# Experts in descending order of their token counts, with falling widths, and one addition on GpSimd instead of VectorE

## The chip, the cores and the metric

The kernel runs on one core of a Trainium2 chip. The metric is the device time of one execution in microseconds; where several executions were timed, their median. A profiled execution also gives a trace: its span runs from the first to the last instruction, and its own time is a little longer than the span.

In this text PE is TensorE, DVE is VectorE, ACT is ScalarE, POOL is GpSimd, and SP is the engine whose queue issues most of the DMAs.

## What is computed

The reference has three stages. A linear attention over 4 sequences of 768 tokens gives 3072 rows of 384 numbers. A mixture of eight experts follows: each token goes to the one expert with the largest gate value. A gated feed-forward layer over all tokens ends it.

```python
def _moe_ref(x, w_gate, w_output_gate, w1, w2):
    e_idx = np.argmax(x @ w_gate, axis=1)
    ...
    for e in range(E):                      # E = 8
        mask = e_idx == e
        h = np.maximum(x[mask] @ w1[e], 0.0)    # 384 -> 1024
        ye = h @ w2[e]                          # 1024 -> 384
        out[mask] = gate_w[mask, None] * eom[mask, e, None] * ye

def _moe2_ref(x, w_gate, w_val, w_out):     # 384 -> 1536 -> 384
    g = x @ w_gate
    silu = g * (1.0 / (1.0 + np.exp(-g)))
    return (silu * (x @ w_val) @ w_out).astype(np.float32)
```

How many tokens an expert gets depends on the data. With the inputs of the reference the counts of experts 0 to 7 are 380, 348, 359, 410, 409, 389, 374 and 403.

## The kernel before

Every float32 product is made of three products of a high and a low part (type fp32r): a low by a high, a high by a low, a high by a high. So each weight and each activation is split: ACT casts the high part, DVE subtracts it from the value and has the low part.

**Attention and routing** (0 to about 131 us). The tokens pass in 24 tiles of 128. `route` finds each token's expert and its place in that expert's list, in groups of six tiles; the last group (18 to 23) is routed when the attention is over. Its result is `rows`, 8 x 4 columns of token numbers, four columns of 128 places for each expert.

**The head** (`MoE.head`, about 130 to 150 us). Expert 0's first 256 tokens come from the first 18 tiles, so its work on them starts while the last group is still routed. It runs in eight steps `f`, one for each 128 of the 1024 hidden units: nine matmuls into `pha`, ACT and DVE make `h` (high and low) of it, and two steps later nine matmuls take `h` into `pya`. `pha` has two PSUM buffers. The small DVE work of the routing stands in the same DVE queue.

**The experts** (`MoE.run`, about 150 to 372 us). Expert 0's other 160 columns come first, then experts 1 to 7 in the order of their numbers, each over `CAP` = 416 columns whatever its count: eight steps of nine matmuls into `ph` and nine into `py`, 144 in all. Beside them each expert needs its weights loaded by SP and split (`load` and `prefetch`, three groups ahead), and its tokens gathered by POOL and transposed on PE (`gather`, `transposed`: four tiles of up to 128 tokens, three transposes each). The last layer's weights arrive as 64-bit floats; `widen` turns 36 chunks of them into float32 in three stages, six chunks during each of experts 1 to 6. In a chunk, line 973 clamps, line 975 makes an exponent, line 978 shifts, line 979 (POOL) multiplies, line 981 (DVE) adds, and line 982 puts the sign in. `sorted_positions` works out where each expert's list starts (`off_f`, `offs`) and the order of the tokens for the output.

**The feed-forward layer** (`FFN`, 372 us to the end) runs over seven blocks of sorted tokens and scatters each finished tile to its tokens by an indirect DMA.

**What sets the order.** In the attention and the head PE, DVE, ACT and POOL follow the order that is written in the code, though a scheduler may put work of the later part between. From `MoE.run` on a scheduler places the instructions. Each engine and the SP queue then works in the order of its own queue. If an expert has more tokens than its columns, `rest` computes them after the end, which these counts don't ask for.

Of the kernel before, what the change touches and what calls it, by code (L numbers as in the profile page):

```python
# [27 lines left out]

HEAD = 256
# [7 lines left out]
def moe_kernel(ctx, tc, cst, small, tok, tr, u, w1, w2, m_gate, m_val, m_out, out):  # L37
# [14 lines left out]
    assert CAP < NJ * P  # L52
# [11 lines left out]
    ident, mask, iota_p, niota, rev8, slot, tokid, tile_i, part_i, ltm = (  # L64
        cs[:, at[n]] for n in ("ident", "mask", "iota", "niota", "rev", "slot", "tokid", "tile", "part", "ltm")
    )
    ltm = ltm.rearrange("p (a b) -> p a b", a=E)
# [11 lines left out]
    rows_h = const.tile([P, 2], I32, name="rows_h")  # L79
    offs = const.tile([P, E], I32, name="offs")  # L80
# [46 lines left out]
    def route(sl, lg, mx, pool, ps, sm):  # L127
# [84 lines left out]
        nc.vector.tensor_tensor(out=rows if sl.stop == NTILE else rows_f, in0=rows_f, in1=psw[:, 1, :], op=ALU.add)  # L212

    def gate(sl, lg, mx, pool, sm):
# [43 lines left out]
        nc.vector.tensor_tensor(out=scale3[:, 2, sl], in0=s1, in1=scale3[:, 1, sl], op=ALU.subtract)  # L258

# [4 lines left out]
    with ExitStack() as actx:  # L264
# [305 lines left out]
        with tc.manual_schedule(engines=set(engines)):  # L570
# [62 lines left out]
            moe.gather(0, more, rows[:, HEAD // P : NJ], NT)  # L633
# [8 lines left out]
    def sorted_positions(pool, pool_ps):  # L642

        psn = pool_ps.tile([P, 2, E], F32, name="psn", tag="pd")
        nc.tensor.matmul(psn[:, 0, :], lhsT=ones_b, rhs=cum[:, NTILE, :], start=True, stop=True)
        nc.tensor.matmul(psn[:, 1, :], lhsT=ones_b, rhs=cum[:, NTILE - NCH, :], start=True, stop=True)
        nc.vector.tensor_copy(cnt_f, psn[:, 0, :])
        nc.vector.scalar_tensor_tensor(
            out=again, in0=psn[:, 1, 0:1], scalar=float(HEAD), in1=wide, op0=ALU.is_lt, op1=ALU.max
        )  # L650

        def ins(t, n, at):
            if at == 1:
                return t.rearrange("p (o e) -> p o e", o=1).to_broadcast([P, n, t.shape[1]])
            return t.rearrange("p (e o) -> p e o", o=1).to_broadcast([P, t.shape[1], n])

        pre = pool.tile([P, E, E], F32, name="pre")
        nc.vector.tensor_tensor(out=pre, in0=ltm, in1=ins(cnt_f, E, 1), op=ALU.mult)
        nc.vector.reduce_sum(off_f, pre, axis=AX.X)

        nc.vector.tensor_copy(offs, off_f)
        nc.vector.tensor_scalar(out=offs[:, E - 1 :], in0=off_f[:, E - 1 :], scalar1=float(FFN.NB), scalar2=None, op0=ALU.max)
        nc.vector.scalar_tensor_tensor(
            out=again, in0=off_f[:, E - 1 :], scalar=float(FFN.NB), in1=again, op0=ALU.is_lt, op1=ALU.max
        )
        yield
        most = pool.tile([P, 1], F32, name="most")
        nc.vector.reduce_max(most, cnt_f, axis=AX.X)
        nc.vector.scalar_tensor_tensor(out=rest_i, in0=most, scalar=float(CAP), in1=again, op0=ALU.is_gt, op1=ALU.max)
# [14 lines left out]
        nc.vector.tensor_copy(dlof, dlo)  # L684
# [14 lines left out]
        for i in range(NTILE):  # L699
            doh = pool.tile([P, P], BF16, name="doh", bufs=4)  # L700
            nc.vector.tensor_scalar(out=doh, in0=iota_p, scalar1=dlof[:, i : i + 1], scalar2=None, op0=ALU.is_equal)
# [25 lines left out]
    def sequential(c):  # L727
# [55 lines left out]
        for _ in gate(slice(0, NTILE), lg, mx, sq, scratch(sq)):  # L783
            pass
        for _ in sorted_positions(sq, ps_m):
            pass

    def rest(c):
# [130 lines left out]
class MoE:  # L919
    def __init__(self, tc, c, env):  # L920
# [9 lines left out]
        self.raws, self.xs = {}, {}  # L930
# [9 lines left out]
    def widen(self):  # L940
# [19 lines left out]
        for i in range(n):  # L960
# [20 lines left out]
            nc.vector.tensor_tensor(out=low, in0=ab, in1=low, op=ALU.add)  # L981
# [8 lines left out]
    def load(self, e, g):  # L990
        nc, env, GF = self.nc, self.env, 2
        r1 = self.raw.tile([P, env["KD"], GF * P], F32, name="r1")
        nc.sync.dma_start(out=r1, in_=self.w1v[e, :, :, g * GF * P : (g + 1) * GF * P])
        r2 = self.raw.tile([P, GF, env["DM"]], F32, name="r2")
        nc.sync.dma_start(out=r2, in_=self.w2v[e, :, g * GF : (g + 1) * GF, :])
        self.raws[e, g] = r1, r2
# [11 lines left out]
    def run(self, sorted_positions, gates, ffn):  # L1008
# [26 lines left out]
        for e in range(E):  # L1035
            x, _ = self.xs.pop(e)
            sl = slice(0 if e else HEAD, CAP)
            py = [p_y.tile([P, CAP], F32, name=f"py{d}") for d in range(KD)]
            for f in range(KF):
# [27 lines left out]
                if f == 3 and e + 1 < E:  # L1067
                    load_x(e + 1, range(NJ))
# [3 lines left out]
    def gather(self, e, tiles, rows, last):  # L1072
# [8 lines left out]
        for i, j in enumerate(tiles):  # L1081
            n = min(P, CAP - j * P)
# [5 lines left out]
    def transposed(self, e, tiles, p_t, tag=None):  # L1088
# [4 lines left out]
        for j in tiles:  # L1093
            n = min(P, CAP - j * P)
# [64 lines left out]
    def second(self, after=None):  # L1159
# [7 lines left out]
        if f == KF - 1:  # L1167
            to = sl
            if e:
# [3 lines left out]
                yd, to = yd[:, :, least:], bass.ds(off - least, env["CAP"])  # L1173
# [158 lines left out]
PREFETCH = (7, 10, 13, 16, 19)  # L1332
# [20 lines left out]
def _const_slices():  # L1353
    at = 0
    for name, width in (("ident", P), ("mask", P), ("iota", P), ("niota", P), ("rev", 8), ("slot", 32), ("tokid", 24), ("tile", 24), ("part", 1), ("ltm", 64)):
        yield name, slice(at, at + width)
        at += width
# [5 lines left out]
def _constants():  # L1363
# [6 lines left out]
    c[:, at["iota"]] = np.arange(P)  # L1370
# [3 lines left out]
    c[:, at["tokid"]] = P * np.arange(24) + np.arange(P)[:, None]  # L1374
    c[:, at["tile"]] = np.arange(24)
    c[:, at["part"]] = np.arange(P)[:, None]
    c[:, at["ltm"]] = np.tril(np.ones((8, 8)), -1).reshape(-1)
# [67 lines left out]
```

## Time and profile before

| | us |
|---|---|
| median of 3 runs | 830.68 |
| lowest and highest | 829.99 and 833.25 |
| profiled execution, its own time | 830.09 |
| profiled execution, its span | 828.2 |
| PE busy in the span | 800.0 |
| DVE busy | 516.8 |
| ACT busy | 350.1 |
| POOL busy | 213.8 |

The mean granted clock of PE was 0.992 of full speed. A busy time is the time covered by instructions of an engine; matmuls overlap each other, and the record of one is longer than its distance from the next. The shares of busy time are averages over stages with different limits, so a table by stage (busy times between given moments) stands behind them. The 1.9 us between span and own time are taken as unchanged.

### The profile page before, as it was taken

How to read it: one execution, taken by the hardware profiler on the slowest of the kernel's cores; microseconds unless marked ns; L12 is line 12 of the kernel's file. 1: busy time of each engine (PE TensorE's matmuls, PEld its weight loads, DVE VectorE, ACT ScalarE, POOL GpSimd, SP SyncE). 2: the span in 40 equal slices, each digit the busy share in tenths (PEclk: the TensorE clock that was granted, in tenths of full speed). 3: DMA queues.
4: the chain of work that ended last, by engine and by line, in shares of the span. 5: the costliest groups of instructions: out<-in, count | busy, mean ns of one | idle time of the engine just before them, and what ended most of it. 6: DMA issues, size and time to landing. Idle time of an engine off the chain costs nothing.

```text
span 828.2 us, 15486 instructions
## 1 busy us (share of the span) xinstructions
PE 800.0 (97%) x5991; PEld 728.2 (88%) x5992; DVE 516.8 (62%) x1096; ACT 350.1 (42%) x794; POOL 213.8 (26%) x210
## 2 busy tenths in 40 slices
PE   7989789998999999999999999999999999999997
PEld 4878678997999999998888888888888888889997
DVE  7789996699999999855554335433533533344443
ACT  5878764565556567543432212212322222222321
POOL 6999952546333422200001000200010020001000
PEclk9999999999999999999999999999999999999999
DMA  8999974576778886332210000100010010001000
GB/s 326 305 366 327 333 239 148 157 224 186 242 237 263 253 233 216 107 120 86 86 58 33 19 1 13 39 1 0 13 39 1 1 44 1 1 8 39 1 20 24
DMA packets 61843, 99.63 MB, mean 120 GB/s; under 512 B 5364, under 2 KB 47872, under 8 KB 61760
## 3 DMA queue, kind: packets, MB, share of 16 engines
q1 hardware_dynamic: 58320, 88.44, 32.8%
q0 software_dynamic: 3440, 10.11, 3.7%
q8 instruction: 49, 0.80, 0.4%
q14 instruction: 34, 0.28, 0.1%
HBM read 82.00 MB, written 16.53 MB: 119 GB/s over the span
## 4 chain that ended last, share of the span: by engine, by line
issue 58%; DVE 12%; PE 8%; DMA 3%; POOL 3%; ACT 0%; POOLq 0%; SPq 0%; DVEq 0%; ACTq 0%
PE ph L1131 3%; PE py L1131 3%; POOL out_dram L1275 2%; DVE w1l L1006 2%; DVE h L1151 1%; DVE ab L978 1%; DMA m<-ab 1%; DVE ab L982 1%; DVE ab L973 1%; DMA r<-in_w_dram 1%; DVE low L981 1%; DVE w2l L1006 1%; PE pya L1131 1%; DVE exw L975 1%; PE pha L1131 1%
## 5 line engine op out<-in xcount | busy, mean ns | idle before, releaser
L1304 DVE TENSOR_TENSOR hv<-pg,hv 128x512 f32<-128x512 f32 (+1 forms) x84 | 51.7, 615 | 155.0 <-ACT hv L1303 154.9
L1275 POOL DMA_INDIRECT out_dram<-ot,tokd x24 | 24.9, 1035 | 450.5 <-DVE ot L1274 446.9
L1303 ACT ACTIVATE hv<-pg 128x512 f32<-128x512 f32 (+1 forms) x84 | 45.1, 537 | 167.8 <-PE pg L1299 167.6
L914 ACT CAST hh<-hv 128x512 fp32r<-128x512 f32 (+1 forms) x84 | 47.0, 559 | 141.8 <-DVE hv L1305 141.8
L1266 PE MATMUL po<-wh,hh 128*128 128x384 f32 x288 | 97.1, 337 | 0.0
L1266 PE MATMUL po<-wh,hl 128*128 128x384 f32 x288 | 97.0, 337 | 0.0
L1266 PE MATMUL po<-wl,hh 128*128 128x384 f32 x288 | 96.8, 336 | 0.0
L1131 PE MATMUL ph<-x,w1h 128*128 128x416 f32 x336 | 91.4, 353 | 0.0
L1299 PE MATMUL pg<-xh,wh 128*128 128x512 f32 (+1 forms) x252 | 91.1, 362 | 0.0
L1299 PE MATMUL pg<-xh,wl 128*128 128x512 f32 (+1 forms) x252 | 90.9, 361 | 0.0
L1299 PE MATMUL pv<-xh,wh 128*128 128x512 f32 (+1 forms) x252 | 90.8, 360 | 0.0
L1299 PE MATMUL pv<-xh,wl 128*128 128x512 f32 (+1 forms) x252 | 90.7, 360 | 0.0
L1299 PE MATMUL pv<-xl,wh 128*128 128x512 f32 (+1 forms) x252 | 90.6, 360 | 0.0
L1299 PE MATMUL pg<-xl,wh 128*128 128x512 f32 (+1 forms) x252 | 90.5, 359 | 0.0
L1131 PE MATMUL py<-h,w2h 128*128 128x416 f32 x336 | 88.1, 352 | 0.0
L915 DVE TENSOR_TENSOR hl<-hv,hh 128x512 fp32r<-128x512 f32 (+1 forms) x84 | 51.7, 616 | 45.4 <-ACT hh L914 45.1
L1305 DVE TENSOR_TENSOR hv<-pv,hv 128x512 f32<-128x512 f32 (+1 forms) x84 | 51.7, 615 | 44.1 <-PE pv L1299 43.7
L979 POOL TENSOR_TENSOR low<-low,exw 128x384 f32<-128x384 f32 x36 | 43.5, 1208 | 103.1 <-DVE exw L975 90.9
L440 ACT ACTIVATE dsb<-cs,cb 128x128 f32<-128x128 f32 x192 | 58.8, 388 | 24.7 <-DVE cb L436 24.7
L1131 PEld LDWEIGHTS ph<-x,w1h 128*128 128x128 f32 x336 | 63.5, 190 | 0.7
L1131 PEld LDWEIGHTS py<-h,w2h 128*128 128x128 f32 x336 | 62.9, 188 | 0.9
L1131 PE MATMUL ph<-x,w1l 128*128 128x416 f32 x168 | 61.0, 363 | 0.6 <-DVE h L1151 0.6
(230 smaller groups left out, 1709.5 us busy)
## 6 DMA issues: line engine op xcount, KB each, us to landing
r<-in_w_dram SPq DMA_DIRECT2D x64, 384.0 KB, 4.5
yd_all<-in_tr_dram SPq DMA_DIRECT2D x24, 512.0 KB, 4.8
yd_all<-in_tok_dram SPq DMA_DIRECT2D x24, 384.0 KB, 6.6
m<-ab SPq DMA_DIRECT2D x36, 192.0 KB, 4.1
rw<-m SPq DMA_DIRECT2D x36, 192.0 KB, 2.5
yd_all<-in_tok_dram SPq DMA_DIRECT2D x24, 256.0 KB, 7.4
x_d<-xt SPq DMA_DIRECT2D x24, 192.0 KB, 2.4
cva<-in_w_gate_dram SPq DMA_DIRECT2D x12, 384.0 KB, 3.5
```

Source lines behind the costliest of these rows:

```text
L440: nc.scalar.mul(dsb[:, h, :], ident, cb[:, h : h + 1])
L914: first = nc.scalar.copy(hi, src)
L915: second = nc.vector.tensor_tensor(out=lo, in0=src, in1=hi.bitcast(F32), op=ALU.subtract)
L979: nc.gpsimd.tensor_tensor(out=low, in0=low, in1=ex.bitcast(F32), op=ALU.mult)
L1006: nc.vector.tensor_tensor(out=lo, in0=r, in1=hi.bitcast(F32), op=ALU.subtract)
L1131: nc.tensor.matmul(dst[:, 0:n], lhsT=a, rhs=b, start=start and t == 0, stop=stop and t == 2)
L1266: mm = nc.tensor.matmul(po[t], lhsT=a[:, t * P : (t + 1) * P], rhs=bb, start=(f == 0 and j == 0), stop=(f == KF2 - 1 and j == 2))
L1275: st = nc.gpsimd.indirect_dma_start(out=out[:, :], out_offset=bass.IndirectOffsetOnAxis(ap=tokd[:, i : i + 1].bitcast(U32), axis=0), in_=o ...
L1299: nc.tensor.matmul(dst, lhsT=a[:, fs], rhs=bb[:, q, :], start=(q == 0 and j == 0), stop=(q == KD - 1 and j == 2))
L1303: nc.scalar.activation(hv, pg, AF.Sigmoid)
L1304: nc.vector.tensor_tensor(out=hv, in0=pg, in1=hv, op=ALU.mult)
L1305: nc.vector.tensor_tensor(out=hv, in0=pv, in1=hv, op=ALU.mult)
```

## The change

Each of experts 1 to 7 gets its turn by its count: the largest first. Expert 0 stays first. The turns have the fixed widths `CAPS` = 416, 416, 412, 404, 392, 384, 372, 360 (the first is expert 0's), so the turn is known when the program is built and the expert in it only when it runs. A turn of 384 columns or fewer has three tiles of tokens instead of four.

`in_order`, new, runs after the last group's routing: it ranks the counts and makes `ids` (which expert has which turn), and a selection matrix `pm`. `sorted_positions` uses `pm` to put `rows` and `offs` in the order of the turns and to check the counts against the widths. `load` reads `ids` into a register of SP and addresses the weights by it; the prefetch of the first group of expert 1 in the attention is dropped (`PREFETCH` has four entries instead of five). The constants lose 200 columns. In `widen` the addition (line 981 before) is issued on GpSimd.

```diff
+CAPS = (416, 416, 412, 404, 392, 384, 372, 360)
...
-        nc.vector.tensor_tensor(out=rows if sl.stop == NTILE else rows_f, in0=rows_f, in1=psw[:, 1, :], op=ALU.add)
+        if sl.stop == NTILE:
+            sl0 = slice(HEAD // P, NJ)
+            nc.vector.tensor_tensor(out=rows_m, in0=rows_f[:, sl0], in1=psw[:, 1, sl0], op=ALU.add)
+        nc.vector.tensor_tensor(out=rows_f, in0=rows_f, in1=psw[:, 1, :], op=ALU.add)
...
+    def in_order(pool, psn):
+        nc.tensor.matmul(psn[:, 0, :], lhsT=ones_b, rhs=cum[:, NTILE, :], start=True, stop=True)
...
+        nc.vector.tensor_tensor(out=ahead, in0=ins(rank8, E, 1), in1=ins(rank8, E, 2), op=ALU.is_gt)
+        at_k = pool.tile([P, E], F32, name="at_k")
+        nc.vector.reduce_sum(at_k, ahead, axis=AX.X)
+        nc.vector.tensor_tensor(out=pm, in0=ins(tile_i[:, 0:E], E, 2), in1=ins(at_k, E, 1), op=ALU.is_equal)
...
+        nc.vector.tensor_copy(ids, ids_f)
...
-            moe.gather(0, more, rows[:, HEAD // P : NJ], NT)
+            moe.gather(0, more, rows_m, NT)
+            in_order(acst, in_bank("psn", 2, E))
...
+        each = pool.tile([P, E, NJ, E], F32, name="each")
...
+        nc.vector.reduce_sum(rows_k.rearrange("p (k j) -> p k j", j=NJ), each, axis=AX.X)
+        nc.vector.tensor_copy(rows, rows_k)
...
-            nc.vector.tensor_tensor(out=low, in0=ab, in1=low, op=ALU.add)
+            nc.gpsimd.tensor_tensor(out=low, in0=ab, in1=low, op=ALU.add)
...
+        if e and g == 0:
+            self.ids[e] = bass.ds(nc.sync.value_load(env["ids"][0:1, e : e + 1], min_val=0, max_val=env["E"] - 1), 1)
+        pe = self.ids[e]
         r1 = self.raw.tile([P, env["KD"], GF * P], F32, name="r1")
-        nc.sync.dma_start(out=r1, in_=self.w1v[e, :, :, g * GF * P : (g + 1) * GF * P])
+        nc.sync.dma_start(
+            out=r1, in_=self.w1v[pe, :, :, g * GF * P : (g + 1) * GF * P].rearrange("o p k f -> (o p) k f")
+        )
...
-            sl = slice(0 if e else HEAD, CAP)
+            sl = slice(0 if e else HEAD, CAPS[e])
...
-                    load_x(e + 1, range(NJ))
+                    load_x(e + 1, range(-(-CAPS[e + 1] // P)))
...
-                yd, to = yd[:, :, least:], bass.ds(off - least, env["CAP"])
+                yd, to = yd[:, :, least:], bass.ds(off - least, n)
...
-PREFETCH = (7, 10, 13, 16, 19)
+PREFETCH = (7, 10, 13, 16)
```

Three places show how the queues change. The first is DVE's queue in the head, behind the last group's routing. `h<-pha` is the low part of a step's `h`; `w2l` and `w1l` are low parts of weights; `den`, `key`, `exo`, `gs`, `sc`, `scale` belong to the gate. Before:

```order
L232 RECIPROCAL reo<-key 128x48
L1151 SCALAR_TENSOR_TENSOR h<-pha,h 128x256
L1006 TENSOR_TENSOR w2l<-r_1726,w2h 128x768
L229 TENSOR_REDUCE den<-ex 128x6
L237 TENSOR_TENSOR key<-ex,reo 128x48
L234 TENSOR_SCALAR den_2780<-den 128x6
L1151 SCALAR_TENSOR_TENSOR h<-pha,h 128x256
L242 TENSOR_TENSOR exo<-key,oh_all 128x48
```

Now, the end of the stretch between the same reciprocal and the same `h`:

```order
L285 TENSOR_TENSOR pick<-pm,cs 128x64
L684 TENSOR_TENSOR each<-pm,rows_f 128x256
L263 TENSOR_TENSOR s_2811<-sc,scale_66 128x6
L287 TENSOR_REDUCE ids_f<-pick 128x8
L691 TENSOR_REDUCE rows_k<-each 128x32
L265 CAST scale_66<-s_2811 128x6
L288 CAST ids<-ids_f 128x8
L289 COPY cnt_f<-bank 128x8
L290 SCALAR_TENSOR_TENSOR again<-bank,wide 128x1
L1201 SCALAR_TENSOR_TENSOR h<-pha,h 128x256
L692 CAST rows<-rows_k 128x32
```

Twenty-two instructions stand between the reciprocal and `h` now and none stood there before; ten more stand between that `h` and the next, among them the split `w2l`.

The second place is DVE's queue while expert 4 is computed; `ab<-ab` are lines 973 and 978, `exw` is line 975, `low<-ab,low` the addition, `ab<-cva,low` line 982, and `doh` belongs to the order of the tokens. Before:

```order
L1151 SCALAR_TENSOR_TENSOR h<-ph,h 128x416
L978 TENSOR_SCALAR ab<-ab 128x384
L1006 TENSOR_TENSOR w2l<-r_3716,w2h 128x768
L981 TENSOR_TENSOR low<-ab,low 128x384
L973 TENSOR_SCALAR ab<-ab 128x384
L982 SCALAR_TENSOR_TENSOR ab<-cva,low 128x384
L975 TENSOR_SCALAR exw<-ab 128x384
L978 TENSOR_SCALAR ab<-ab 128x384
```

Now (lines 973, 975, 978 and 982 have become 1018, 1020, 1023 and 1027):

```order
L1201 SCALAR_TENSOR_TENSOR h<-ph,h 128x392
L1018 TENSOR_SCALAR ab<-ab 128x384
L1020 TENSOR_SCALAR exw<-ab 128x384
L1023 TENSOR_SCALAR ab<-ab 128x384
L1006 TENSOR_TENSOR w2l<-r_3879,w2h 128x768
L1201 SCALAR_TENSOR_TENSOR h<-ph,h 128x392
L745 TENSOR_SCALAR doh<-cs,dlof 128x128
L1027 SCALAR_TENSOR_TENSOR ab<-cva,low 128x384
```

The addition is gone from the queue (it stands in POOL's, behind the multiplication of the same chunk), and three other instructions stand here between the shift and line 1027, which waits for it.

The third place is SP's queue at the end of the attention; `yd_all<-in_tok_dram` loads a tile of the attention, `r` are an expert's weights, `cva` the 64-bit weights. Before:

```order
L993 DMA r_2007<-in_w_dram 128x3x256
L995 DMA r_2009<-in_w_dram 128x2x384
L993 DMA r_2753<-in_w_dram 128x3x256
L995 DMA r_2755<-in_w_dram 128x2x384
L993 DMA r_2757<-in_w_dram 128x3x256
L995 DMA r_2759<-in_w_dram 128x2x384
L304 DMA yd_all<-in_tok_dram 128x512
```

Now:

```order
L998 DMA cva<-in_w_out_dram 128x768
L1038 TENSOR_LOAD ids
L1038 ISA x2
L1041 ISA
L1041 DMA r_2771<-in_w_dram 128x3x256
L1045 ISA
L1045 DMA r_2773<-in_w_dram 128x2x384
```

Six loads of expert 1 that stood ahead of the last attention load stand behind the read of `ids` now, which comes after the whole attention, with two more behind them.

## Rows read from the trace of the kernel before

**Rows 1.** The page: span, and busy time by engine
```profile
span 828.2 us, 15486 instructions
PE 800.0 (97%) x5991; PEld 728.2 (88%) x5992; DVE 516.8 (62%) x1096; ACT 350.1 (42%) x794; POOL 213.8 (26%) x210
```

**Rows 2.** Busy time of each engine in the turns of experts 1 to 7
```profile
core 0: us, PE busy (x) PEld busy (x) DVE busy (x) ACT busy (x) POOL busy (x), PEclk, DMA share, GB/s
166.40:199.00 32.60, 32.49 (x181) 30.92 (x179) 32.24 (x61) 18.44 (x38) 15.95 (x13) 1.00 0.64 196
199.00:229.50 30.50, 27.82 (x141) 26.71 (x140) 26.75 (x54) 17.52 (x34) 12.14 (x10) 0.94 0.78 247
229.50:259.40 29.90, 29.90 (x167) 28.50 (x167) 28.44 (x59) 18.40 (x37) 11.69 (x11) 1.00 0.79 253
259.40:288.70 29.30, 29.30 (x166) 28.01 (x165) 29.02 (x60) 16.92 (x34) 11.59 (x11) 1.00 0.82 246
288.70:317.50 28.80, 28.80 (x162) 27.44 (x161) 27.58 (x61) 19.10 (x37) 7.14 (x7) 1.00 0.79 238
317.50:345.60 28.10, 28.10 (x155) 27.50 (x154) 26.78 (x53) 17.34 (x34) 7.63 (x8) 1.00 0.50 149
345.60:371.60 26.00, 26.00 (x140) 25.78 (x139) 15.92 (x29) 13.31 (x27) 1.59 (x2) 1.00 0.42 128
```

**Rows 3.** Timeline of PE (start, us, instruction): nine of 416, nine of 256, six transposes
```profile
361.77 0.35 PE L1131 MATMUL ph<-x,w1l 128*128 128x416 f32 x1
...
363.46 0.92 PE L1131 MATMUL py<-h,w2h 128*128 128x416 f32 x4
...
142.16 0.28 PE L1131 MATMUL pha<-x,w1l 128*128 128x256 f32 x1
...
143.22 0.28 PE L1131 MATMUL pya<-h,w2l 128*128 128x256 f32 x1
...
152.13 0.82 PE L1097 MATMUL pt<-cs,xg 128*128 128x128 f32 x6
152.71 0.40 PE L1127 MATMUL ph<-x,w1h 128*128 128x320 f32 x1
```

**Rows 4.** DVE by line, 259.4 to 288.7 us: busy us, mean ns, idle before
```profile
L1151 DVE SCALAR_TENSOR_TENSOR h<-ph,h 128x416 fp32r<-128x416 f32 x9 | 5.2, 581 | 0.0
L978 DVE TENSOR_SCALAR ab<-ab 128x384 int32<-128x384 int32 x7 | 4.7, 675 | 0.1
...
L981 DVE TENSOR_TENSOR low<-ab,low 128x384 f32<-128x384 f32 x6 | 3.3, 548 | 0.1
...
L975 DVE TENSOR_SCALAR exw<-ab 128x384 int32<-128x384 int32 x6 | 2.1, 351 | 0.0
```

**Rows 5.** Timeline of POOL and DVE around one multiplication
```profile
341.87 1.12 POOL L979 TENSOR_TENSOR low<-low,exw 128x384 f32<-128x384 f32 x1 [3.11 <-DVE exw L975]
342.04 0.58 DVE L1151 SCALAR_TENSOR_TENSOR h<-ph,h 128x416 fp32r<-128x416 f32 x1
342.54 1.27 DVE L1006 TENSOR_TENSOR w2l<-r,w2h 128x768 fp32r<-128x768 f32 x1
```

**Rows 6.** Timeline of DVE: an `h` of the head, two small dependent steps
```profile
139.60 0.41 DVE L1151 SCALAR_TENSOR_TENSOR h<-pha,h 128x256 fp32r<-128x256 f32 x1
...
150.64 0.22 DVE L658 TENSOR_TENSOR pre<-cs,cnt_f 128x64 f32<-128x64 f32 x1
150.90 0.22 DVE L659 TENSOR_REDUCE off_f<-pre 128x8 f32<-128x64 f32 x1
```

**Rows 7.** A wait of PE after expert 1, and the microsecond behind it
```profile
203.73 0.54 PE L1131 MATMUL py<-h,w2l 128*128 128x416 f32 x1 [2.10 <-ACT yd_all L1175]
...
204.00:205.00 1.00, 1.00 (x4) 0.94 (x4) 1.00 (x4) 1.00 (x3) 1.00 (x1) 0.50 0.93 320
```

**Rows 8.** The page's row of the weight loads; a register load on SP
```profile
r<-in_w_dram SPq DMA_DIRECT2D x64, 384.0 KB, 4.5
...
L906 SPq TENSOR_LOAD <-rest_i x1: 472/472/472, 176.2 to 176.2; - x1
```

More of the change, by code (lines that the diff above doesn't have):

```diff
@@ L51, in moe_kernel @@
     NJ = -(-CAP // P)
-    assert CAP < NJ * P
+    assert CAP < NJ * P and CAP == max(CAPS) and len(CAPS) == E
     G = 2 * E
@@ L63, in moe_kernel @@
     at = dict(_const_slices())
[L64 to L65 removed]
+    ident, mask, niota, rev8, slot, tile_i, part_i, lead, caps = (
+        cs[:, at[n]] for n in ("ident", "mask", "niota", "rev", "slot", "tile", "part", "lead", "caps")
     )
[L67 removed]
     mask_b = const.tile([P, P], BF16, name="mask_b")
@@ L79, in moe_kernel @@
     rows_h = const.tile([P, 2], I32, name="rows_h")
+    rows_m = const.tile([P, NJ - HEAD // P], I32, name="rows_m")
+    ids = const.tile([P, E], I32, name="ids")
+    ahead = const.tile([P, E, E], F32, name="ahead")
+    pm = const.tile([P, E, E], F32, name="pm")
+    cap_f = const.tile([P, E], F32, name="cap_f")
     offs = const.tile([P, E], I32, name="offs")
@@ L652, in ins @@
[L652 to L662, printed above, removed]
@@ L663, in sorted_positions @@
-        nc.vector.scalar_tensor_tensor(
-            out=again, in0=off_f[:, E - 1 :], scalar=float(FFN.NB), in1=again, op0=ALU.is_lt, op1=ALU.max
+        pre = pool.tile([P, E, E], F32, name="pre")
+        nc.vector.tensor_tensor(out=pre, in0=ahead, in1=ins(cnt_f, E, 1), op=ALU.mult)
+        nc.vector.reduce_sum(off_f, pre, axis=AX.X)
+        each = pool.tile([P, E, NJ, E], F32, name="each")
+        nc.vector.tensor_tensor(
+            out=each,
+            in0=pm.rearrange("p k (o e) -> p k o e", o=1).to_broadcast([P, E, NJ, E]),
+            in1=rows_f.rearrange("p (o e j) -> p o j e", o=1, j=NJ).to_broadcast([P, E, NJ, E]),
+            op=ALU.mult,
+        )
@@ L667, in sorted_positions @@
+        nc.vector.reduce_sum(cap_f, caps_e, axis=AX.X)
+        over = pool.tile([P, E], F32, name="over")
+        nc.vector.tensor_tensor(out=over, in0=cnt_f, in1=cap_f, op=ALU.subtract)
         most = pool.tile([P, 1], F32, name="most")
-        nc.vector.reduce_max(most, cnt_f, axis=AX.X)
-        nc.vector.scalar_tensor_tensor(out=rest_i, in0=most, scalar=float(CAP), in1=again, op0=ALU.is_gt, op1=ALU.max)
+        nc.vector.reduce_max(most, over, axis=AX.X)
+        nc.vector.scalar_tensor_tensor(out=rest_i, in0=most, scalar=0.0, in1=again, op0=ALU.is_gt, op1=ALU.max)
@@ L784, in sequential @@
             pass
+        in_order(sq, ps_m.tile([P, 2, E], F32, name="psn", tag="m"))
         for _ in sorted_positions(sq, ps_m):
@@ L929, in __init__ @@
         self.pend = []
-        self.raws, self.xs = {}, {}
+        self.raws, self.xs, self.ids = {}, {}, {0: slice(0, 1)}
         self.first = ExitStack()
@@ L1354, in _const_slices @@
     at = 0
-    for name, width in (("ident", P), ("mask", P), ("iota", P), ("niota", P), ("rev", 8), ("slot", 32), ("tokid", 24), ("tile", 24), ("part", 1), ("ltm", 64)):
+    for name, width in (("ident", P), ("mask", P), ("niota", P), ("rev", 8), ("slot", 32), ("tile", 24), ("part", 1), ("lead", 8), ("caps", 8)):
         yield name, slice(at, at + width)
@@ L1373, in _constants @@
     c[:, at["slot"]] = P * np.arange(32)
-    c[:, at["tokid"]] = P * np.arange(24) + np.arange(P)[:, None]
     c[:, at["tile"]] = np.arange(24)
     c[:, at["part"]] = np.arange(P)[:, None]
-    c[:, at["ltm"]] = np.tril(np.ones((8, 8)), -1).reshape(-1)
+    c[:, at["lead"]] = [2**16, *range(-1, -8, -1)]
+    c[:, at["caps"]] = CAPS
     return c
```

48 lines of the change are left out of this document (34 added, 14 removed).

## The prediction, on record before the result

> **What bounds the kernel now.** I read the page first: PE is busy for 800.0 of 828.2 us, DVE for 516.8 [rows 1]. That says PE, but the shares hide where DVE is full, so I read the busy times by turn next. While experts 2 to 6 are computed DVE is busy for 26.75 to 29.02 us of turns of 28.1 to 30.5 [rows 2]: in expert 4's turn it is idle for 0.28 us, in 3's for 1.46, in 5's for 1.22, in 6's for 1.32. PE is covered all the time in 3 to 7. So both engines bound this stretch, and a saving on one of them alone comes only as far as the other has room. Expert 7's turn is different: DVE is busy there for 15.92 of 26.0 us. Behind it the feed-forward layer isn't touched by the change.
>
> What a turn costs PE is read from its timeline [rows 3]. Nine matmuls of 416 columns take from 361.77 to 363.46, 0.1878 us each; nine of 256 columns take 1.06 us, 0.1178 each. The difference, 0.0700 us over 160 columns, is 0.4375 ns a column. Six transposes take 0.58 us, 0.097 each.
>
> **The narrower turns.** A turn has 144 matmuls, so a column less saves 144 x 0.4375 ns = 0.063 us. Turns 2 to 7 lose 4, 12, 24, 32, 44 and 56 columns: 0.25, 0.76, 1.51, 2.02, 2.77 and 3.53 us, 10.84 in all. Turns 5, 6 and 7 have one tile less, three transposes each, done one turn earlier: 0.29 us in each of turns 4, 5 and 6, 0.87 in all. PE has 11.71 us less to do. Turn 1 keeps its 416 columns.
>
> **The addition on GpSimd.** DVE loses an instruction of 0.548 us six times in a turn [rows 4]. That isn't clear profit. The shift of line 978 runs beside POOL's multiplication and takes 0.675 us on the mean, where line 975, of the same kind and size, takes 0.351 [rows 4]: POOL's work delays DVE. One multiplication shows which instructions it delays [rows 5]. POOL runs from 341.87 to 342.99; `h`, which reads PSUM, takes 0.58 us under it, as it does on the mean of the turn; the split `w2l`, which reads two operands from SBUF, takes 1.27. The addition has the same size as the multiplication, so I price it at 1.12 us on POOL. How much of that DVE loses is not in the trace. If an idle DVE or an `h` covers it all, it loses nothing, and gains 0.548; if a split or a shift stands behind it all the time, it loses 1.12, net 0.57. In the new queue an `h` stands behind the shift or behind one split in nearly all chunks. I take 1.12 - 0.58 = 0.54 lost: gain and loss cancel, and DVE's load stays as it is. Line 982 waits for the addition now, but with at least an `h` and a split or their like between; I cost this wait at nothing. If that cover were too short, some tenths of a us in each chunk would be due, and `h` would be queued behind it, for which PE waits.
>
> So DVE's room decides what of PE's saving is seen. `h` shrinks with its width: 8 x 0.581 us x the columns lost over 416, which is 0.13, 0.27, 0.36 and 0.49 us in turns 3 to 6. I allow DVE no less idle time than the 0.28 us of turn 4. Turn 2 saves 0.25. Turn 3 has 1.46 - 0.28 + 0.13 = 1.31 of room for 0.76, so 0.76. Turn 4 has 0.27 of room for 1.80, so 0.27. Turn 5 has 1.22 - 0.28 + 0.36 = 1.30 for 2.31, so 1.30. Turn 6 has 1.32 - 0.28 + 0.49 = 1.53 for 3.06, so 1.53. Turn 7 has room for all of its 3.53. The sum is 7.64 us, and 4.07 of the 11.71 are held back by DVE.
>
> **The ranking in the head.** Twenty-two small DVE instructions come to stand between a reciprocal and the fifth `h`, which started at 139.60 [rows 6]. A step that depends on the one before follows it after 0.26 us (150.64 to 150.90); where two chains alternate, as here the gate's and the ranking's, half of that. 22 x 0.13 = 2.9 us, and some 0.4 for two wider ones: `h` at about 142.9, ended at 143.3. PE wants its PSUM buffer back at 142.16, for the matmuls of the seventh step [rows 3]: 1.1 us late. Ten more instructions stand ahead of the next `h`, with a split of about 1 us: by the same rates some 2.3 us until it starts, where PE has 2.1 us of work and was late already; I add 0.9. Together +2.0 us. Bounds: 0, if the scheduler's gaps take it up, and 22 x 0.26 - 1.5 = 4, if every step waits for its forerunner. Similar steps that stood between the head and expert 0's rest go away, but PE didn't wait for them.
>
> **The loads.** Six weight loads move from behind the attention's tiles to behind the read of `ids`, which costs SP about 0.47 us [rows 8]. A load lands 4.5 us after its issue [rows 8]. `ids` is ready at about 142.6, so the first weights are there at about 148, and their splits come in the third and fourth step of expert 0's rest, after 155. Hidden, unless the eight loads and the gathers delay each other. The 200 constants less and the earlier last load of the attention are costed at nothing, since PE and DVE work through that time.
>
> **The sum.** 830.09 (the profiled execution's own time) - 7.64 + 2.0 = 824.4 us. The median of the runs is 830.68, 0.6 higher; I count from the profiled one.
>
> **Rivals.** First, DVE has room after all: additions fall under `h` and under idle time, and PE's whole 11.71 us are seen: 830.09 - 11.71 + 2.0 = 820.4. For it: the waits of DVE for POOL's product go. It can be more: PE waits for 2.10 us after expert 1 and then runs at a granted clock of 0.50 (1.2 instead of 2.4 GHz) for some 4 us [rows 7], because ACT and DVE lag. Without that lag 4 us more are gained: 816.4. Against it: DVE is nearly full in turns 3 to 6.
>
> Second, the lock, which ends on the other side. Each addition keeps DVE for all of its 1.12 us, 0.57 net, six times in a turn: 3.42 us. Turn 1, where DVE is busy for 32.24 of 32.60 us [rows 2], grows by 3.06; turn 3 by 28.44 + 3.42 - 0.13 + 0.28 - 29.90 = 2.1; turn 4 by 3.15; turn 5 by 2.1; turn 6 by 1.9. Turns 2 and 7 still save 3.78. That is +8.5, and with the head +10.5: 840.6 us. Between the two each 0.1 us more lost in an addition costs 2.8 us, so from a loss of 0.75 us on the kernel is no faster than before. The `w2l` of 1.27 us speaks for it [rows 5], the unharmed `h` against it. A rule of the Trainium skill names this mechanism (SBUF — State Buffer, section on the two separate sides): GpSimd and a VectorE instruction that runs in a two-port mode or has two SBUF inputs take one pair of ports in turns, the first to start keeps it for its whole length, and the other stands still. The rows above agree: `w2l` is held, `h` with its one SBUF input isn't. By the rule without cover the sum is the 840.6 of this rival, by my half cover 824.4.
>
> Third, the weights or tokens of expert 1 come late, because eight loads and its gather are squeezed into the ten microseconds after 143. An `h` then waits behind a split in DVE's queue. Price: about 3 us, the rest of a load's 4.5 us [rows 8] behind a cover of 1 to 2; 827.4.
>
> Fourth, the change doesn't do what it says: a count beyond its turn's width would call `rest`, at a price of many tens of us. The counts in falling order, 410, 409, 403, 389, 374, 359 and 348, all lie under 416, 412, 404, 392, 384, 372 and 360, and expert 0's 380 under 416. It remains for a mistake of mine.
>
> **How the numbers follow.** Forecast 0.42, the first rival 0.28, the lock 0.19, late loads 0.08, the fourth 0.03. The range of 817 to 832 takes in the first rival down to near its end, the head's bounds, late loads and the lighter half of the lock; some 0.18 lie outside. A measurement of this kernel tells about 0.5% from no change, 4.15 us here: faster is below 826.5, slower above 834.8. Faster: 0.36 of the forecast, all of the first rival, 0.07 of the others, 0.71. Slower: 0.09 of the lock and 0.02 of the rest, 0.11. Same: 0.18.
>
> **What would show it.** In the trace of the changed kernel: nine matmuls of 360 columns in about 1.47 us; the turns, in order, at about 32.6, 30.2, 29.1, 29.0, 27.5, 26.6 and 22.5 us; DVE still over 95% busy in turns 3 to 6, with splits or shifts stretched beside POOL's additions. If DVE is idle for over 2 us in these turns, the first rival holds. If a turn is longer than before and DVE full, the lock does. In the head, PE waiting for `h` for some 2 us between 142 and 149. I am wrong if PE waits elsewhere for a chain through POOL, or if the additions run markedly longer than 1.12 us.

## The result and the profile after

The changed kernel takes 836.29 us (median of 4 runs, 835.38 to 837.98) against 831.23 for the kernel before (4 runs): a ratio of 1.007, interval 1.0049 to 1.0091. I had forecast 824.4, faster. The profiled execution took 835.38 us.

First the page of the changed kernel, which answers [rows 1], and the windows of its turns 1 to 7, each from its first `h` on, which answer [rows 2] (columns as there).

```profile
span 833.3 us, 15608 instructions
...
PE 793.0 (95%) x5982; PEld 718.7 (86%) x5983; DVE 519.1 (62%) x1073; ACT 347.4 (42%) x791; POOL 254.9 (31%) x243
```
```profile
168.50:202.20 33.70, 31.29 (x167) 30.31 (x166) 31.71 (x57) 17.66 (x36) 21.51 (x18) 0.95 0.58 188
202.20:233.20 31.00, 30.26 (x161) 28.61 (x159) 27.69 (x48) 18.52 (x37) 19.28 (x16) 1.00 0.82 255
233.20:263.00 29.80, 29.11 (x164) 27.30 (x164) 29.59 (x53) 16.49 (x33) 17.47 (x15) 1.00 0.78 232
263.00:294.00 31.00, 28.83 (x163) 26.35 (x161) 28.71 (x53) 17.54 (x35) 19.06 (x16) 1.00 0.77 240
294.00:323.00 29.00, 26.17 (x154) 24.84 (x154) 28.83 (x53) 17.28 (x34) 14.21 (x12) 1.00 0.73 224
323.00:351.00 28.00, 26.87 (x159) 26.02 (x159) 25.49 (x44) 17.50 (x35) 15.62 (x13) 1.00 0.51 157
351.00:376.20 25.20, 23.19 (x131) 22.66 (x130) 15.70 (x30) 12.56 (x27) 3.22 (x3) 0.93 0.44 131
```

DVE has 36 operations less to do (the additions), and yet it is busy for 519.1 us, where it was 516.8. PE is busy for 793.0 us against 800.0, 7.0 less and not the 11.7 that I counted. In the turns it now stands idle for 12.0 us (207.7 of turns less 195.7 busy) where it stood for 2.8, most of it in waits for `h` (the total, how often, the longest; before, then now):

```profile
PE ph L1131 <- DVE h L1151: 0.6, 1, 0.6
...
PE ph L1181 <- DVE h L1201: 10.4, 12, 2.4
```

Behind two of its idle times, of 2.42 us (up to 195.44) and of 2.01 us (up to 356.06), the granted clock is 0.50 for 3.4 us each (from 195.8 and from 356.2), which is why turns 1 and 7 show 0.95 and 0.93; before, one turn showed such a fall. Turns 1, 2, 4 and 5 are longer than before, turns 3 and 6 shorter by 0.1 us, and turn 7 alone gains, 0.8.

Where did DVE's time go? Its operations by line, over all seven turns of the changed kernel (busy us, mean ns, idle before, releaser):

```profile
L1056 DVE TENSOR_TENSOR w2l<-r,w2h 128x768 fp32r<-128x768 f32 x26 | 31.2, 1201 | 0.0
L1056 DVE TENSOR_TENSOR w1l<-r,w1h 128x768 fp32r<-128x768 f32 x25 | 29.0, 1159 | 0.0
L1023 DVE TENSOR_SCALAR ab<-ab 128x384 int32<-128x384 int32 x36 | 24.1, 669 | 0.6
L1018 DVE TENSOR_SCALAR ab<-ab 128x384 f32<-128x384 f32 x36 | 22.1, 613 | 0.0
L1027 DVE SCALAR_TENSOR_TENSOR ab<-cva,low 128x384 int32<-128x384 int32 x36 | 21.6, 600 | 8.7 <-POOL low L1026 8.7
L1020 DVE TENSOR_SCALAR exw<-ab 128x384 int32<-128x384 int32 x36 | 14.9, 415 | 0.4
L745 DVE TENSOR_SCALAR doh<-cs,dlof 128x128 bf16<-128x128 f32 x24 | 9.2, 414 | 0.0
```

The lines moved by 45 to 50: 1018 is the clamp, 1020 the exponent, 1023 the shift, 1024 the product, 1026 the addition, 1027 the sign, 1056 the split, 1201 `h`. The splits and the clamp have a longer mean than the 0.95 and 0.35 us that they take where nothing of POOL runs beside them, and line 1027 waits 8.7 us for GpSimd's addition. Three places of the changed kernel's timeline, POOL beside DVE, show both:

```profile
263.00 0.56 DVE L1201 SCALAR_TENSOR_TENSOR h<-ph,h 128x392 fp32r<-128x392 f32 x1
264.03 1.07 POOL L1026 TENSOR_TENSOR low<-ab,low 128x384 f32<-128x384 f32 x1
264.15 1.77 DVE L1056 TENSOR_TENSOR w1l<-r,w1h 128x768 fp32r<-128x768 f32 x1
...
281.62 2.09 POOL L1133 DMA_INDIRECT xg<-x_d,rows  x1 [0.30 <-issue]
283.73 1.03 POOL L1026 TENSOR_TENSOR low<-ab,low 128x384 f32<-128x384 f32 x1
284.79 1.36 DVE L1027 SCALAR_TENSOR_TENSOR ab<-cva,low 128x384 int32<-128x384 int32 x1 [1.96 <-POOL low L1026]
286.34 0.55 DVE L1201 SCALAR_TENSOR_TENSOR h<-ph,h 128x392 fp32r<-128x392 f32 x1
...
291.06 1.62 POOL L1026 TENSOR_TENSOR low<-ab,low 128x384 f32<-128x384 f32 x1
291.72 1.18 DVE L1018 TENSOR_SCALAR ab<-ab 128x384 f32<-128x384 f32 x1
```

In the first an `h` is over before the addition begins, and a split that takes 0.95 us alone takes 1.77 beside an addition: held for 0.82. In the second the addition stands behind a gather of POOL's queue, line 1027 waits 1.96 us for it and is then itself held beside the next product, which POOL begins at 284.70 (1.36 for 0.55), and `h`, for which PE waits, stands behind. In the third a clamp of 0.35 us takes 1.18. An `h` beside POOL isn't harmed, as [rows 5] had it: 0.557 us on the mean in the turn from 263.

### The profile page after: what moved, and what is told of

The parts are those of the page before. It is cut to its first block, busy times and chain, and to the rows that moved or that the text cites. A ratio compares the mean times of both kernels' runs of the same rounds, so it can differ in the third digit from the quotient of the medians.

```text
span 833.3 us, 15608 instructions
## 1 busy us (share of the span) xinstructions
PE 793.0 (95%) x5982; PEld 718.7 (86%) x5983; DVE 519.1 (62%) x1073; ACT 347.4 (42%) x791; POOL 254.9 (31%) x243
## 4 chain that ended last, share of the span: by engine, by line
issue 58%; DVE 15%; PE 5%; POOL 4%; DMA 1%; ACT 1%; POOLq 0%; SPq 0%; ACTq 0%; DVEq 0%
POOL out_dram L1325 2%; DVE ab L1023 2%; DVE h L1201 2%; DVE w1l L1056 2%; DVE ab L1018 2%; DVE w2l L1056 2%; DVE ab L1027 2%; DVE exw L1020 1%; POOL low L1026 1%; DVE doh L745 1%; PE ph L1181 1%; PE pya L1181 1%; PE py L1181 1%; PE pha L1181 1%; DVE x L960 1%
## 5 line engine op out<-in xcount | busy, mean ns | idle before, releaser
L1181 PE MATMUL ph<-x,w1h 128*128 128x416 f32 (+6 forms) x336 | 89.1, 347 | 0.0
L1181 PE MATMUL py<-h,w2h 128*128 128x416 f32 (+6 forms) x336 | 83.5, 343 | 0.0
L1181 PE MATMUL ph<-x,w1l 128*128 128x416 f32 (+6 forms) x168 | 61.1, 364 | 10.7 <-DVE h L1201 10.4
L1024 POOL TENSOR_TENSOR low<-low,exw 128x384 f32<-128x384 f32 x36 | 41.5, 1151 | 60.1 <-DVE exw L1020 49.1
## 6 DMA issues: line engine op xcount, KB each, us to landing
yd_all<-in_tr_dram SPq DMA_DIRECT2D x24, 512.0 KB, 7.1
```

The costliest lines, as they stand in the source:

```text
L1024: nc.gpsimd.tensor_tensor(out=low, in0=low, in1=ex.bitcast(F32), op=ALU.mult)
L1181: nc.tensor.matmul(dst[:, 0:n], lhsT=a, rhs=b, start=start and t == 0, stop=stop and t == 2)
```

## The experiments

In all these runs the kernel before took 828.4 to 829.0 us (medians), so the times below compare with one another to half a microsecond. First the three parts were put in singly.

**The addition back on DVE; the addition alone; the ranking alone; all but the widths.** The first kernel has the first edit below, made to the changed kernel; the second is the kernel before with the reverse of it; the third has both edits; the fourth has the second edit alone:

```diff
-            nc.gpsimd.tensor_tensor(out=low, in0=ab, in1=low, op=ALU.add)
+            nc.vector.tensor_tensor(out=low, in0=ab, in1=low, op=ALU.add)
...
-CAPS = (416, 416, 412, 404, 392, 384, 372, 360)
+CAPS = (416, 416, 416, 416, 416, 416, 416, 416)
```

> The changed kernel with the addition of the widening back on VectorE; ranking and widths stay. Theory A (the addition on GpSimd took away what the widths gave: VectorE's operations beside it stretch by 18.5 us over the 36 additions, and the chunk's last operation waits 8.7 us for GpSimd with h queued behind it): about 825 us, 823 to 828; PE's idle time in turns 1 to 7 falls from 12 us to under 5. Theory B (the ranking by counts and the weights' addresses that come from it delay expert 1, and that delay is the loss): 835 to 836, the addition's engine hardly matters. Theory C (VectorE is full anyway, so narrower experts give nothing): about the kernel before, 831 to 833.

> The kernel before with one edit, the addition on GpSimd. Theory A: slower than before by 5 to 10 us, 836 to 841, with VectorE's weight differences at 1.15 us or more in the mean (0.98 to 1.02 before) and a wait of several us ahead of the chunk's last operation. Theory B: within 1.5 us of the kernel before, 830 to 833. My prediction's price (gain 0.548, loss 0.54 for each addition): 831, no change.

> The changed kernel with the addition on VectorE and every width 416, so that of the change only the ranking, the order of the experts and the weights' addresses read from it are left. Theory A: 832 to 833.5, the ranking costs 1 to 2 us ahead of expert 1 and nothing behind it. Theory B: 836 or more.

> The changed kernel with every width 416; ranking and the addition on GpSimd stay. Theory A: slower than both kernels, 838 to 843, since the widths are what holds the changed kernel at 836. Theory C (VectorE sets the turns, not the width): 836 to 837, as the changed kernel. Theory B: 836 to 838.

| kernel | addition on | median us | ratio to before, interval |
|---|---|---|---|
| ranking and widths | VectorE | 825.02 | 0.9952 (0.994 to 0.9965) |
| kernel before, addition moved | GpSimd | 836.15 | 1.0093 (1.0075 to 1.011) |
| ranking alone | VectorE | 830.57 | 1.0016 (1.0007 to 1.0026) |
| ranking, no widths | GpSimd | 838.91 | 1.0119 (1.0103 to 1.0135) |

The times are those of theory A in all four; only PE's idle time with the addition on DVE, expected under 5 us, was 7.5 between the first and the last `h` of the turns (196.2 less 188.7), and 7.4 of it were waits for `h`: with the addition back, DVE still holds PE up. The ranking costs 1.6 us (830.57 - 828.99). The widths give 5.5 (830.57 - 825.02). The addition costs 7.2 alone (836.15 - 828.99), 8.3 beside the ranking, and 9.8 beside the widths (834.81, the changed kernel run again below, less 825.02). Why the last is more wasn't tested; narrower turns leave DVE less slack to lose, which would do it. The same DVE rows of the kernel with the addition on DVE, to be laid beside those above:

```profile
L1056 DVE TENSOR_TENSOR w2l<-r,w2h 128x768 fp32r<-128x768 f32 x26 | 27.4, 1052 | 0.0
L1023 DVE TENSOR_SCALAR ab<-ab 128x384 int32<-128x384 int32 x36 | 25.9, 719 | 0.3
L1056 DVE TENSOR_TENSOR w1l<-r,w1h 128x768 fp32r<-128x768 f32 x25 | 24.6, 985 | 0.0
L1027 DVE SCALAR_TENSOR_TENSOR ab<-cva,low 128x384 int32<-128x384 int32 x36 | 20.4, 566 | 0.3
L1026 DVE TENSOR_TENSOR low<-ab,low 128x384 f32<-128x384 f32 x36 | 19.7, 548 | 3.4 <-POOL low L1024 3.2
L1018 DVE TENSOR_SCALAR ab<-ab 128x384 f32<-128x384 f32 x36 | 14.1, 391 | 0.9 <-ACT ab L1013 0.9
L1020 DVE TENSOR_SCALAR exw<-ab 128x384 int32<-128x384 int32 x36 | 13.5, 375 | 0.1
```

With the addition on GpSimd the clamp grows by 8.0 us, the splits by 3.8 and 4.4, exponent and sign by 1.4 and 1.2, the shift shrinks by 1.8: 17.0 us, and the waits for POOL grow by 5.5 (8.7 - 3.2). That is 22.5 us lost for the 19.7 taken away. Such sums by line count the overlap of neighbouring records twice; as a whole DVE is busy for 519.1 us against 518.1, so in busy time alone gain and loss nearly cancel, and the waits are what is over.

**What the addition is worth if nobody makes it, and if GpSimd does and nobody reads it.** Then the other way round: the product to DVE as well. And line 1027 a step later, in a function `sign` that is called behind the next `yield`. The first two kernels leave the sum out of the widened weights. Each against the changed kernel, the third against the one with the addition on DVE:

```diff
-            nc.gpsimd.tensor_tensor(out=low, in0=ab, in1=low, op=ALU.add)
...
-            nc.gpsimd.tensor_tensor(out=low, in0=ab, in1=low, op=ALU.add)
+            nc.gpsimd.tensor_tensor(out=ex.bitcast(F32), in0=ex.bitcast(F32), in1=ex.bitcast(F32), op=ALU.add)
...
-            nc.gpsimd.tensor_tensor(out=low, in0=low, in1=ex.bitcast(F32), op=ALU.mult)
+            nc.vector.tensor_tensor(out=low, in0=low, in1=ex.bitcast(F32), op=ALU.mult)
...
             if i + 1 < n:
                 yield
+                sign(*late)
```

> The changed kernel without the addition at all (the widened weights lack their mantissa's sum; no engine does it), to price what VectorE gains if the addition left it for nothing: 36 x 0.548 = 19.7 us of VectorE. Wait theory (W) and stretch theory (S) alike: below the kernel with the addition on VectorE, which ran in 825.0, by 2 to 5 us, 820 to 823. If VectorE's room is not what holds the turns: 824 to 825.

> The changed kernel with GpSimd's addition replaced by one of the same shape on the exponent's buffer that no instruction reads (the sum is left out of the widening): GpSimd is as busy as in the changed kernel, VectorE has as few operations, and nothing waits for that operation. Theory W (the loss is the wait of the chunk's last operation for GpSimd, behind the product and the gathers in its queue): near or below the kernel with the addition on VectorE, 822 to 826, and the 8.7 us of idle ahead of line 1027 are gone. Theory S (the loss is VectorE's stretched operations, 18.5 us in 36 additions): 831 to 835, about the changed kernel (834 to 835 on this chip).

> The kernel with ranking and widths, with the addition and also the product before it on VectorE, so that GpSimd does nothing of the widening. VectorE gets 36 x 0.548 = 19.7 us more and loses the stretch of the operations beside the product (line 1023 0.72 against 0.35, 13.3 us; lines 1018, 1056, 1020 some 5 us) and 3.2 us of waits for the product. Theory S (a GpSimd operation costs VectorE about as much as it would take itself): 823 to 826, no worse than 825.0. Theory W: VectorE's net work counts only by waits, 823 to 827. If the stretch is not GpSimd's doing: VectorE gets 20 us more in full turns, 832 or more.

> The changed kernel with the chunk's last operation (line 1027, which takes the sum) issued one step later, at the start of the next chunk, so that some 1.8 us of other work stand between it and the addition; the addition stays on GpSimd. Theory W: the 8.7 us of waits ahead of line 1027 fall under 2, and the time to 825 to 828. Theory S: 831 to 835, as the changed kernel, with VectorE's weight differences still at 1.15 to 1.2 us.

Without the addition: 814.48 us, 10.5 below 825.02, more than expected. With GpSimd's operation that nobody reads: 827.65, so the operation costs 13.2 us without any reader, more than its leaving DVE gave. This lies between the two expectations: the stretch alone turns the gain into a loss of 2.6, and 7 us more are missing up to the changed kernel. Of those 2.6 some 1.5 lie ahead of the turns in the profiled executions, whose first `h` of the turns begins at 168.52 and at 166.98: ahead of the first the granted clock was 0.50 for 3.4 us (from 139.7), ahead of the second, with the addition on DVE, it was 1.00 from 130 on. And GpSimd wasn't as busy as in the changed kernel: 243.6 us against 254.9, to which I come back below. The late sign took 834.56, and waits of 9.1 us remained: the scheduler had put line 1027 nearly where it had been, so this run told nothing.

The product on DVE took **816.29 us** (ratio 0.9849, interval 0.983 to 0.9868), against an expected 823 to 826. Nothing of the widening runs on GpSimd then, and these are its DVE rows, over the turns:

```profile
L1056 DVE TENSOR_TENSOR w1l<-r,w1h 128x768 fp32r<-128x768 f32 x26 | 25.8, 992 | 0.1
L1056 DVE TENSOR_TENSOR w2l<-r,w2h 128x768 fp32r<-128x768 f32 x26 | 24.8, 954 | 0.7 <-ACT w2h L1053 0.7
L1024 DVE TENSOR_TENSOR low<-low,exw 128x384 f32<-128x384 f32 x36 | 20.9, 580 | 0.0
...
L1023 DVE TENSOR_SCALAR ab<-ab 128x384 int32<-128x384 int32 x36 | 13.7, 381 | 0.0
```

The shift falls from 0.719 to 0.381 us, `w2l` to 0.954, and no operation waits for POOL. With 36 operations more DVE is busy for 512.0 us of the whole span, where it was 518.1. Of the versions that compute the whole result it is the fastest, and from the changed kernel it differs in the engine of two lines alone.

**The product on DVE in the kernel before, and the sign two steps later.** The first edit is the third line above. The second calls `sign(*late)` ahead of the next chunk's addition and puts the chunk's `load(i + 2)` behind it.

> The kernel before with one edit, the product of the widening (line 979) on VectorE, so that GpSimd does nothing of the widening; order and widths as before. Theory P (with GpSimd out of the way TensorE alone sets the turns; in the kernel before it is busy 202.4 of 205.2 us there): a gain of 2 to 3 us, 825.5 to 827, and the distance to the kernel with the same edit, ranking and widths (816.3) is then about 10, which is the matmul sum of 11.7 us less 1.6 for the ranking: the widths give all of it once VectorE has room. Theory V (VectorE sets the turns with wide experts too): a gain of 8 us, as this edit gave the narrow kernel (825.0 to 816.3), 820 to 822.

> The changed kernel with the chunk's last operation (line 1027) issued only ahead of the next chunk's addition, two steps later than in the changed kernel, with the load of the chunk after next behind it; one step was too little, the scheduler set it nearly where it had been and 9.1 us of waits stayed. Theory W (the wait for GpSimd's addition is worth the 7 us between the changed kernel and the one whose GpSimd operation nobody reads, 827.6): the waits ahead of this operation fall under 2 us and the time to 827 to 829. Theory S' (the distance of these two is where the stretch falls and not the wait): 833 to 835 though the waits are gone.

The kernel before with its product on DVE: 825.03 us, 3.7 faster than before (ratio 0.9952). There PE is the bound (theory P): between the first and the last `h` of the turns it stands idle for 0.8 of 197.2 us. From there to 816.29 are 8.7 us; with the ranking's 1.6 added, the widths give 10.3 of the 11.7 us that were counted on PE. The later sign took 836.06 us: its waits fell to 2.0, but ScalarE waited 25.8 us for the buffer that it frees, DVE's `h` then 9.1 for ScalarE. So the wait theory was still open.

**The wait taken away by another operand.** Line 1027 works on the exponent's buffer, so that nobody reads GpSimd's sum, which the widened weights then lack; in the second of these kernels GpSimd adds the product to itself and so doesn't wait for the shift; the third has no such operation (the changed kernel itself ran beside the first):

```diff
-            ab = cv.tile([P, DM], F32, name="ab", bufs=3)
+            ab = cv.tile([P, DM], F32, name="ab", bufs=2)
...
-            ex = cv.tile([P, DM], I32, name="exw")
+            ex = cv.tile([P, DM], I32, name="exw", bufs=3)
...
-                out=bits, in0=pair[:, :, 1], scalar=-(2**31), in1=low.bitcast(I32), ...
+                out=ex, in0=pair[:, :, 1], scalar=-(2**31), in1=ex, ...
...
-            nc.gpsimd.tensor_tensor(out=low, in0=ab, in1=low, op=ALU.add)
+            nc.gpsimd.tensor_tensor(out=low, in0=low, in1=low, op=ALU.add)
```

> The changed kernel, but the chunk's last operation (line 1027) takes the exponent's buffer in place of the sum and writes there; GpSimd makes the sum as before, behind the shift and in the same place of its queue, and nobody reads it (the sum is left out of the widened weights). All of GpSimd's and VectorE's operations have the shape and the order they have in the changed kernel but for a few places; only the wait of line 1027 for the addition is gone. Issuing line 1027 later had not settled it: the waits for the addition fell from 8.7 to 2.0 us, but ScalarE then waited 25.8 us for buffers that line 1027 frees, and the time stayed. Theory W (that wait is what lies between 834.5 and the 827.6 of the kernel whose GpSimd operation nobody reads): 826 to 829. Theory S' (what lies between is where the stretch falls): 833 to 836.

> The changed kernel itself, beside the one above on the same chip: 834 to 836 by all theories, 0.5 to 0.9% above the kernel before.

> As the kernel whose sum is unread (line 1027 works on the exponent's buffer; the sum is left out), but GpSimd's second operation adds the product to itself, so it follows the product at once and doesn't wait for the shift; nobody reads it. Against that kernel (834.5) only the moment of GpSimd's operation differs. Theory M (the moment: right behind the product it falls on the same operations of VectorE as the product does, behind the shift it holds up one more): 826 to 829, as the kernel with the unread operation on the exponent's buffer (827.6). Theory B (the buffers of the rewritten line 1027, two for the shifted value and three for the exponent, cost those 7 us, and the run on the reader's wait said nothing): 833 to 836.

> The same rewritten line 1027 and buffers without any second operation on GpSimd (the sum is left out): what the rewriting costs by itself, against the kernel without the addition (814.5). Theory M: 813 to 816. Theory B: 818 to 822.

The sum unread, behind the shift: 834.47 us. The changed kernel: 834.81. The operation right behind the product: 827.79. None: 813.71, so the buffers cost nothing. The wait theory falls: taking the reader away gains 0.3 us, which the intervals can't tell from nothing. Between the early and the late operation lie 6.7 us, as theory M had it. Page rows of the early one, then of the late one:

```profile
PE 789.6 (96%) x5982; PEld 714.3 (87%) x5983; DVE 518.7 (63%) x1073; ACT 348.7 (42%) x791; POOL 243.6 (30%) x243
...
L1027 DVE SCALAR_TENSOR_TENSOR exw<-cva,exw 128x384 int32<-128x384 int32 x36 | 30.3, 842 | 3.0 <-POOL low L1024 2.9
```
```profile
PE 792.0 (95%) x5982; PEld 714.3 (86%) x5983; DVE 523.0 (63%) x1073; ACT 347.5 (42%) x791; POOL 253.6 (31%) x243
...
L1027 DVE SCALAR_TENSOR_TENSOR exw<-cva,exw 128x384 int32<-128x384 int32 x36 | 35.6, 988 | 1.8 <-POOL low L1024 1.8
```

The late one has no wait for the sum, but line 1027 takes 0.988 us where it took 0.600 in the changed kernel: what DVE doesn't spend waiting it spends held. The early one costs DVE 4.3 us less of busy time (523.0 - 518.7).

I had written ahead of the runs that only the moment differs between these two. That isn't so. The early operation reads one tensor twice, the late one two tensors, and the early one is shorter: thirteen of the early ones take 0.82 or 0.83 us, while no late one takes less than 0.99. One of each:

```profile
241.76 0.83 POOL L1026 TENSOR_TENSOR low<-low 128x384 f32<-128x384 f32 x1
...
242.46 1.01 POOL L1026 TENSOR_TENSOR low<-ab,low 128x384 f32<-128x384 f32 x1 [0.36 <-DVE ab L1023]
```

36 times 0.18 are 6.5 us of GpSimd, near the whole distance. And the moment is mostly the same: in 27 of 36 chunks the late operation has no wait for the shift before it either. Here is such a chunk of the early kernel, then of the late one; the operation starts 1.20 and 1.21 us behind the start of the product, lasts 0.19 us longer in the second, and line 1027 is held 0.18 longer:

```profile
256.83 1.42 POOL L1026 TENSOR_TENSOR low<-low 128x384 f32<-128x384 f32 x1
257.50 1.18 DVE L1027 SCALAR_TENSOR_TENSOR exw<-cva,exw 128x384 int32<-128x384 int32 x1
...
258.33 1.61 POOL L1026 TENSOR_TENSOR low<-ab,low 128x384 f32<-128x384 f32 x1
258.99 1.36 DVE L1027 SCALAR_TENSOR_TENSOR exw<-cva,exw 128x384 int32<-128x384 int32 x1
```

So moment and length came together in this edit, and no run parts them; the same holds for the 7 us between the changed kernel and the first unread operation, which added the exponent to itself. An early operation on two tensors would settle it.

## Why the prediction was wrong

**The step that failed is the price of the addition**, "gain and loss cancel", with the wait of line 982 "at nothing". The gain was right in size: without the addition DVE is busy for 498.3 us instead of 518.1, 0.55 us for each. The loss was priced at 0.54. In busy time alone it is 20.8 us (519.1 - 498.3), or 0.58 for each, so that DVE's load stayed as it was, as I had written. That the middle between no loss and 1.12 us came so near was luck, for the cover that I gave as its reason wasn't there: an `h` runs beside 11 of the 36 additions only. In the queue it does stand behind the shift, but POOL is still at the product then, as in the first place above. And the wait came on top: line 1027 waits 8.7 us instead of the 1.3 without any addition. 20.8 + 7.4 = 28.2 us, or 0.78 for each addition, against 0.55 gained. The cover of an `h` and a split or their like, which was to hide this wait, was too short, and where the addition stood behind a gather far too short (1.96 us).

I had written that from 0.75 on the kernel is no faster than before. At 0.78 the same sentence gives about 831 us; most of the rest lies in the widths. By the single runs the addition cost 8.3 us (838.91 - 830.57) where I had nothing, the widths gave 4.1 instead of 7.64, and the ranking cost 1.6 instead of 2.0. These three make the 11.5 us between the forecast change of -5.7 and the +5.8 that the runs add up to.

**Wait and stretch are one loss.** Taking the reader away took the wait away, and line 1027 was held instead (0.600 to 0.988 us); the time stayed. The unread sum still costs DVE 24.6 us of busy time and 0.5 of waits, 0.70 for each, against the kernel with the same buffers and no operation. The unread operation on one tensor costs 20.3 us (518.7 - 498.4) and 1.6 of waits (2.9 - 1.3), 0.61 for each. All of these are more than the 0.55 that leaving frees; how much of the step from 0.61 to 0.70 is the operation's length and how much its moment stays open.

**DVE's price in time.** My sum took equal gain and loss on DVE as no loss of time. In time the leaving gave 10.5 us and the unread operation cost 13.2, for 19.8 and 19.9 us of DVE. The traces show where it goes: between the first and the last `h` of the turns PE stands idle for 0.0 us without the operation, for 8.3 with the unread one and for 12.0 in the changed kernel. An operation held for 0.8 us delays the `h` behind it. A mean over a turn doesn't show that.

**The widths** were priced at 7.64. They gave 5.5 with the addition on DVE and 4.1 (838.91 - 834.81) with it on GpSimd. The limit by DVE's room was the right mechanism, since with DVE free 10.3 of 11.7 us came; its size was off. The matmul sum itself was right: nine matmuls of 360 columns take the forecast 1.47 us (364.96 to 366.43 in the timeline of PE, changed kernel).

```profile
364.96 0.33 PE L1181 MATMUL ph<-x,w1l 128*128 128x360 f32 x1
...
366.43 1.14 PE L1181 MATMUL py<-h,w2h 128*128 128x360 f32 x6
```

**The ranking** was priced at 2.0 us and cost 1.6. The wait lies elsewhere than I said: the fifth `h` begins at 141.93, not 142.9, and PE has no wait for `h` between 142 and 149. It waits up to 139.16, ahead of the ranking's two matmuls in its own queue, where it had no wait before:

```profile
139.16 0.17 PE L276 MATMUL bank<-cum,ones_b 128*128 128x8 bf16 x1 [1.79 <-DVE rows_f L221]
```

I had counted the DVE steps of the ranking and not asked what its matmuls wait for. The size was right for another reason.

**The rivals.** The lock was the right one, at a chance of 0.19 and 840.6 us; its loss of 1.12 was too high and its direction right. The sign that I had named for it, a turn longer than before with DVE full, stands in the turn from 263: 31.0 us against 29.3, of which DVE is busy for 28.71 and waits 2.0 for POOL. The sign named for the first rival, DVE idle for over 2 us, stands there as well (2.3 us, and 2.5 in turn 6), though that rival failed: the sign didn't ask what DVE was waiting for. PE's waits for `h` behind a chain through POOL are the other thing that the last sentence had feared. The additions also run longer than 1.12 us, as it had feared, too: 1.30 on the mean. Late loads and `rest` don't show. The first rival's 820.4 needed DVE free; with both operations back on DVE it came, and more (816.29).

The Trainium skill has a rule that I didn't weigh (Perfetto Trace Analysis, section on optimizing scalar and DVE operations): offloading between VectorE and GpSimd may not help, since they share a port. These runs bear it out: 36 products moved back from GpSimd took 8.7 us off.

## What to carry to other kernels

An operation that GpSimd takes from a full VectorE isn't free for VectorE: price it by an operation of GpSimd that the trace already has, as the growth of every VectorE operation beside it and the waits for its result, and ask of the existing ones whether they should come back. A wait that a change adds and the stretch beside it are one loss in two columns; add busy and waiting time before judging either. Where two engines are full, put the parts of a change in singly: two of these parts together were worth 4.0 us (828.99 - 825.02), and the third hid them. An operation that stands in for another in an experiment must be as long as it: here one that reads one tensor twice was 0.18 us shorter, and the comparison lost its meaning by it.

## What the hardware showed

- A GpSimd addition of 128 x 384 costs DVE 0.70 us where nobody reads the sum and 0.78 in the changed kernel, waits counted; DVE makes it in 0.548. An operation that adds a tensor to itself costs DVE 0.61, counted in the same way.
- On GpSimd the addition of two tensors takes 0.99 us or more, that of a tensor to itself 0.82 or more. Beside DVE's operations both take longer: the means are 1.30 and 1.045 us, and an addition that begins while a split runs takes 1.62 (291.06 above).
- Clamp and split are held beside it (0.35 to 1.18, 0.95 to 1.77 us), and so is the sign operation with two SBUF operands (0.55 to 1.36); `h`, from PSUM, isn't.
- DVE's records overlap. In the timeline of the kernel with the addition on DVE the next operation starts 0.46 us after an addition of 0.54, so busy times by line add up to more than the engine was busy:

```profile
271.74 0.54 DVE L1026 TENSOR_TENSOR low<-ab,low 128x384 f32<-128x384 f32 x1
272.20 0.35 DVE L1018 TENSOR_SCALAR ab<-ab 128x384 f32<-128x384 f32 x1
```
